# Adding transfers, one load queue and an earlier mask in the front of a fused attention and gated-convolution kernel

## The chip, the cores and the metric

The kernel runs on one core of a Trainium2 chip, in one launch. The metric is the device time of that launch in microseconds. Times before: 495.88 us median of 3 runs, 494.71 to 499.05.

## The reference

q, k and v are 4 x 8 x 576 x 64 (batch, head, position, width) in single precision. Each head adds two attentions: a pooled one, on q, k, v averaged over groups of 4 positions (144 of them), its result repeated 4 times; and a local one, where a position sees only keys less than 4 away. The 8 heads are joined to x, 4 x 576 x 512. Then two gated layers, their weights in double precision:

```
out_d = sm_attn(q_d, k_d, v_d)                       # q_d = mean of 4 rows, and so on
scores = np.where(abs(i - j) < 4, scale * q @ k.T, -1e9)
x = repeat(out_d, 4) + softmax(scores) @ v
h = relu(x @ w_in);  x = (h * sigmoid(conv3(h))) @ w_out          # 512 -> 1024 -> 512
out = (sigmoid(conv5(x)) * (x @ w_val)) @ w_out2                  # 512 -> 512 -> 512
```

## The kernel before

Attention is done in 16 steps (4 batches x 4 pairs of heads). A step loads k and q (`load`), turns them on TensorE (`transp`), copies them out of PSUM on ScalarE (`evac`), pools them on VectorE (`pooled`), and runs the pooled attention (`down_s` to `down_o`) and the local one (`loc_s` to `loc_o`). Local scores are made in blocks of 24 positions by 32 keys; the mask is a tile that TensorE adds first (`loc_s`, `identr` times `maskr`). GpSimd makes the mask (lines 832 to 848: one memset, twelve selections), and VectorE copies it to `maskr`. Local values come as windows of v in `ldw` tiles (`load_vw`, for the first batch `load_vw_first`: 24 transfers of 64 KB, 12 from SP, 12 from GpSimd). Pooled v is made by `pool_v`: one load of all four rows of a group, two additions on VectorE.

The large products take every operand as a high and a low part and sum three products (`mm3`). The high part is a ScalarE copy to the short format, the low part what is left of the value, subtracted on VectorE (`parts`; for weights `Weights.pieces`). A weight block of 512 columns by 128 rows is loaded as double precision into a stage (`Weights.load`, four stages, later three, in tiles that batches 1 to 3 use later on), and turned to single precision by one ScalarE and four VectorE instructions (`sign_off`, `to_f32`); then come the high part and the low part. There are 16 such blocks for `win` and `wout`. The first four are loaded from SP's queue, the other twelve from GpSimd's, each as soon as its stage is free.

The order of the work is written out by hand for the first four steps: `FRONT` is a list of piece names (tpk0: transpose k of step 0; pv: pool v; ab, cv, hi, lo: the four pieces of a weight block; xn, xo: the two halves of a step's output sum), and `ordered` keeps TensorE, VectorE and ScalarE in that order. GpSimd's and SP's instructions aren't held by it, they are placed by the framework's scheduler. Behind the list, steps 4 to 15 run in 8 slots each (`att_slots`), and after every slot `due_at` says how many units of the two layers' products (`ab_units`: for each batch 16 units A, x by w_in, then 16 units B, by w_out) have to have been issued. At the units in `SPLITS` the next weight block is converted and another load is issued. Behind step 15 only products of the layers are left.

Loads of the first batch go to tiles of their own; from the second batch on, `ldk`, `ldq`, `ldw` and `ldv` have one buffer each. k, q and v of step 4 are loaded ahead of `FRONT` and once more by the pieces of step 3.

Of the kernel before, what the change touches and what calls it, by code (L numbers as in the profile page):

```python
# [63 lines left out]
def kernel(  # L64
# [89 lines left out]
            return call  # L154

    vec, act = Noted(nc.vector, "vec"), Noted(nc.scalar, "act")

    def ordered(fn, engines=("pe",)):

# [31 lines left out]
    class Weights:  # L191
# [5 lines left out]
            self.staged = []  # L197
            self.n = 0

        def load(self, queue=nc.gpsimd):  # L200
            if not self.jobs:
                return
            dst, src, r0, nr, c0 = self.jobs.pop(0)
            wide = PW // nr
            rows = src[r0 * 128 : (r0 + nr) * 128]
            t, w = self.stage(self.n)
            self.n += 1
            if src.dtype == F32:
                queue.dma_start(
                    out=w.rearrange("p (r n) -> p r n", r=nr),  # L210
                    in_=rows.rearrange("(r p) n -> p r n", p=128)[:, :, c0 : c0 + wide],
                )
            else:
                queue.dma_start(
                    out=t.rearrange("p (r n) -> p r n", r=nr),
                    in_=rows.bitcast(I32).rearrange("(r p) n -> p r n", p=128)[
                        :, :, 2 * c0 : 2 * (c0 + wide)
                    ],
                )
            self.staged.append((t, w, src.dtype == F32, dst, r0, nr, c0))  # L220
# [7 lines left out]
        def pieces(self, job):  # L228
            t, w, plain, dst, r0, nr, c0 = job
            hi, lo = (d[:, r0 : r0 + nr, c0 : c0 + PW // nr] for d in dst)  # L230
            wr = w.rearrange("p (r n) -> p r n", r=nr)
            words = t.rearrange("p (n t) -> p n t", t=2)
            return (
                lambda: plain or sign_off(act, w, words),
                lambda: plain or to_f32(vec, w, words),
                lambda: act.activation(out=hi, in_=wr, func=AF.Copy),
                lambda: vec.tensor_tensor(out=lo, in0=wr, in1=hi.bitcast(F32), op=ALU.subtract),
            )


    actx = ExitStack()
    ap = actx.enter_context(tc.tile_pool(name="ap", bufs=2))
    T, Y = {}, {}

    def load_v(b, hp):
        t = ap.tile([HD, 2, 2, 4, D], F32, tag="ldv", name="ldv", bufs=1)
        nc.sync.dma_start(
            out=t.rearrange("p e s r d -> p e s (r d)"),
            in_=v[b, 2 * hp : 2 * hp + 2].rearrange("h (s p r) d -> p h s (r d)", s=2, r=4),
        )  # L250
        T["ldv", b, hp] = t

    first = {}

    def load(src, tag, b, hp):

        if b == 0:
            slot = f"hg{'hi' if tag == 'ldk' else 'lo'}{hp}"
            t = mp.tile([QT, 2, NT, D], F32, tag=slot, name=tag)
            nc.sync.dma_start(  # L260
                out=t.rearrange("p e t d -> p e (t d)"),
                in_=src[b, 2 * hp : 2 * hp + 2].rearrange("h (p t) d -> p h (t d)", p=QT),
            )
        else:
            t = ap.tile([QT, NT, 2, D], F32, tag=tag, name=tag, bufs=1)
            for e in range(2):
                nc.sync.dma_start(
                    out=t[:, :, e, :], in_=src[b, 2 * hp + e].rearrange("(t p) d -> p t d", p=QT)
                )
        T[tag, b, hp] = t  # L270

    def load_v_first(part):

        if part == 0:
            first["v"] = keep.tile([HD, H, 2, 4, D], F32, tag="wout1", name="ldv")
        n = H // 2
        t = first["v"][:, part * n : part * n + n]
        nc.sync.dma_start(
            out=t.rearrange("p h s r d -> p (h s) (r d)"),
            in_=v[0, part * n : part * n + n].rearrange("h (s p r) d -> p (h s) (r d)", s=2, r=4),  # L280
        )
        for hp in range(part * HP // 2, (part + 1) * HP // 2):
            T["ldv", 0, hp] = first["v"][:, 2 * hp : 2 * hp + 2]

    def load_vw_first(queue, blocks):

# [32 lines left out]
    ROWS = [slice(64 * e, 64 * e + 64) for e in range(2)]  # L319

    def pool_v(s):
        b, hp = where(s)
        vq = T.pop(("ldv", b, hp))
        t2 = vq[:, :, :, 0:2]
        vec.tensor_tensor(out=t2, in0=t2, in1=vq[:, :, :, 2:4], op=ALU.add)
        vd = ap.tile([HD, 2, 2, D], F32, tag="vd", name="vd")
        vec.tensor_tensor(out=vd, in0=t2[:, :, :, 0], in1=t2[:, :, :, 1], op=ALU.add)
        T["vd", s] = vd

    def transp(s, name):  # L330
        src = T.pop(("ld" + name, *where(s)))
        p = pair("tp")
        inrow = src.shape[1] == 2
        for i in range(NT):
            to = p[:, i // 3, i % 3 * QT : i % 3 * QT + QT]
            if inrow:
                for e in range(2):
                    mm(to[ROWS[e]], src[:, e, i], ident[:QT, :QT], start=True, stop=True)
            else:
                mm(to, src[:, i].rearrange("p e d -> p (e d)"), ident[:QT, :QT], is_transpose=True)  # L340
        T["tp" + name, s] = p, inrow

    def evac(s, name):
        p, inrow = T.pop(("tp" + name, s))
        t = ap.tile([128, S], F32, tag=name + "T", name=name + "T", bufs=1)
        if inrow:
            to = t.rearrange("c (p s i) -> c p s i", s=2, i=3)
            pv = p[:, :, : 3 * QT].rearrange("c s (i p) -> c p s i", i=3)
        else:
            to, pv = t.rearrange("c (s p) -> c s p", s=2), p[:, :, : 3 * QT]  # L350
        act.activation(out=to, in_=pv, func=AF.Copy, scale={"k": scale, "q": 1.0}[name])
        T[name + "T", s] = t
# [202 lines left out]
    def where(s):  # L555
        return s // HP, s % HP

    def att_slots(s):
# [22 lines left out]
            put(7, s, down_av, down_o)  # L581
        if s + 1 < NSTEP:
            put(4, s + 1, lambda s: prep(s, "k"), lambda s: load_vw(*where(s)))
            put(5, s + 1, lambda s: prep(s, "q"), pool_v, next_v)
        return P

    XO = []

    def next_load(s, name):
        if HP <= s + 1 < NSTEP:  # L590
            load({"k": k, "q": q}[name], "ld" + name, *where(s + 1))

    def next_v(s):
        if HP <= s + 1 < NSTEP:
            load_v(*where(s + 1))

    def prep(s, name):
        transp(s, name)
# [226 lines left out]
    for hp in range(2):  # L825
        load(k, "ldk", 0, hp)
        load(q, "ldq", 0, hp)
    load_v_first(0)
    load_vw_first(nc.sync, (0, 1))
    for h in HT:  # L830
        nc.gpsimd.memset(h, 0.0)
    nc.gpsimd.memset(mask, 0.0)
    m3 = mask[:, : NG * KB].rearrange("p (g k) -> p g k", k=KB)
    spans = [(c, 0, NG, 4) for c in range(4)]
    spans[0] = (0, 1, NG - 1, 4)
# [1 line left out]
    for c, g, n, off in spans + [(0, 0, 1, 0), (3, NG - 1, 1, QB * (NB - 1) - key_start(NB - 1))]:  # L837
        m = m3[32 * c : 32 * c + 32, g : g + n]
        for sgn in (1, -1):
            nc.gpsimd.affine_select(  # L840
                out=m,
                in_=m,
                compare_op=ALU.is_ge,
                fill=BIG,
                base=3 - sgn * off,
                pattern=[[0, n], [sgn, KB]],
                channel_multiplier=-sgn,
            )
    vec.tensor_copy(identr, ident)
    vec.tensor_copy(maskr, mask)  # L850
    load_vw_first(nc.gpsimd, (2, 3))

    def stage(n):
        tag = ("y1", "y2", "y3", "g")[n % 4] if n < 9 else ("y2", "y3", "g")[n % 3]
# [9 lines left out]
    for hp in range(2, HP):  # L864
        load(k, "ldk", 0, hp)
        load(q, "ldq", 0, hp)
        if hp == 2:
            load_v_first(1)
    for _ in range(4):
        W.load(nc.sync)  # L870
    nw = 3 * KF + 5 * KM
# [13 lines left out]
        T["cw"] = pair("cw")[:, 0]  # L885
        mm(T["cw"][:, :nw], cwf, ident[:nw, :nw], is_transpose=True)

    load_v(1, 0)
    load(k, "ldk", 1, 0)
    load(q, "ldq", 1, 0)  # L890
    stream = [fn for b in range(B) for fn in ab_units(b)]
# [3 lines left out]
    def due_at(n):  # L895
# [4 lines left out]
        if n > 32:  # L900
            return n
        n += 4
        return n * 16 // 14 if n < 14 else 16 + (n - 14) * 16 // 22

    def step_unit():

# [21 lines left out]
                behind(conv5_e, 1, e)  # L928

    ALL = ("pe", "vec", "act")  # L930
    SPLITS = (0, 2, 4, 6, 8, 10, 12, 14, 16, 18, 20, 22)
    FRONT = """
        tpk0 tpq0 kT0 kd0 qT0 pv0 sl0 qd0 pv1 sd0 mxl0 tpq1 mxd0 sub0 xd0 tpk1 qT1 smd0 scd0 qd1
        kT1 etd0 xl0 kd1 sl1 sml0 etc0 mul0 tr0 sd1 mxl1 sub1 avd0 mxd1 xl1 sml1 xd1 tpq2 mul1 pv2
        od0 avl0 qT2 smd1 scd1 qd2 avm0 xn0 tpk2 xo0 tr1 xhi0 xlo0 etd1 kT2 kd2 sl2 etc1 ab0 cv0
        sd2 avd1 mxd2 hi0 tpq3 ab1 mxl2 xd2 sub2 lo0 pv3 od1 tpk3 qT3 xl2 smd2 qd3 ab2 scd2 sml2
        avl1 mul2 kT3 etd2 xn1 kd3 ab3 avm1 cv1 etc2 sd3 xo1 hi1 sl3 mxd3 xhi1 tr2 xd3 xlo1 avd2
        mxl3 cwa0 smd3 tpk4 od2 sub3 scd3 cv3 avl2 xl3 kT4 avm2 xn2 hi3 etd3 sml3 xo2 tpq4 etc3
        mul3 xhi2 tr3 avd3 cv2 qT4 od3 avl3 cwv0 hi2 avm3 xn3 xlo2 cwp0 xo3 cwc0 xhi3 lo3 xlo3 lo2
        lo1 pv4 qd4 kd4  # L940
    """.split()

    def by_name():

        F = {}
        for s in range(HP + 1):
            for name, fn in dict(
                tpk=lambda s: (transp(s, "k"), next_load(s, "k"), load_vw(*where(s)) if s == HP else 0),
                tpq=lambda s: (transp(s, "q"), next_load(s, "q")),
                kT=lambda s: evac(s, "k"),  # L950
                qT=lambda s: evac(s, "q"),
                kd=lambda s: pooled(s, "k"),
                qd=lambda s: pooled(s, "q"),
                pv=lambda s: (pool_v(s), next_v(s)),
                sl=loc_s,
                mxl=loc_m,
                sub=loc_d,
# [118 lines left out]
```

## Time and profile before

| | |
|---|---|
| median of 3 runs | 495.88 us (494.71 to 499.05) |
| profiled execution | 497.79 us, its span 496.0 us, granted TensorE clock 0.921 |
| TensorE products busy | 449.8 us (91%) |
| TensorE weight loads busy | 415.2 us (84%) |
| VectorE busy | 362.0 us (73%) |
| ScalarE busy | 266.4 us (54%) |
| GpSimd busy | 22.1 us (4%) |
| DMA | 39.59 MB in 69620 packets, mean 80 GB/s |
| chain that ended last | TensorE 58%, VectorE 23%, ScalarE 9%, DMA 5%, issue 4% |

Busy times of matmuls are modelled, so a TensorE that is 91% busy is not at 91% of its peak. A share over the whole span mixes stages with different limits; the chain of waits and the busy times of single stretches tell them apart. In the rows, PE is TensorE, PEld its weight loads, DVE VectorE, ACT ScalarE, POOL GpSimd, and SPq, POOLq the queues that issue transfers. Nearly all instructions carry the line of a helper (L141, L151), so a piece is known by the tiles it writes and reads.

### The profile page before, as it was taken

The page shows a single profiled execution, that of the slowest core. Times are in us where ns is not written, and L with a number is a line of the kernel's source. Part 1 is how long each engine was busy: PE and PEld are TensorE (multiplying, and loading weights), DVE is VectorE, ACT ScalarE, POOL GpSimd, SP SyncE. Part 2 cuts the span into 40 slices and gives each one's busy share as a digit, 9 for nine tenths or more (in the row PEclk, how much of TensorE's full clock was granted, in tenths as well). Part 3 has the DMA queues.
Part 4 walks back from the last instruction along what each step waited for, and adds up shares of the span by engine and source line. Part 5 has one row for each costly group of instructions (what it writes and reads, how often), then busy time and mean ns, then how long its engine had stood idle before and what let it go on. Part 6 is the DMA issues. An engine that isn't in the chain of part 4 may idle for free.

```text
span 496.0 us, 13820 instructions
## 1 busy us (share of the span) xinstructions
PE 449.8 (91%) x5961; PEld 415.2 (84%) x5961; DVE 362.0 (73%) x655; ACT 266.4 (54%) x564; POOL 22.1 (4%) x49
## 2 busy tenths in 40 slices
PE   3669995987798999999999999999979999999997
PEld 3469885976698998987999988899979999889985
DVE  0588998999976458898857998338999775939530
ACT  2357637677554356784654976426684443635221
POOL 7200010101100000000000000000000000000000
PEclk9985558878777999999999999999999999999999
DMA  9994443424341431413314121142101000210102
GB/s 192 204 256 121 84 155 93 130 64 111 113 123 29 97 78 32 104 29 78 79 35 100 36 48 34 34 166 91 44 1 44 0 1 21 86 65 22 65 23 106
DMA packets 69620, 39.59 MB, mean 80 GB/s; under 512 B 55978, under 2 KB 64502, under 8 KB 69558
## 3 DMA queue, kind: packets, MB, share of 16 engines
q1 hardware_dynamic: 67446, 31.62, 25.3%
q0 software_dynamic: 2112, 7.08, 4.6%
q8 instruction: 47, 0.77, 0.6%
q14 instruction: 15, 0.12, 0.1%
HBM read 33.96 MB, written 4.72 MB: 78 GB/s over the span
## 4 chain that ended last, share of the span: by engine, by line
PE 58%; DVE 23%; ACT 9%; DMA 5%; issue 4%; POOL 1%; POOLq 0%; DVEq 0%; ACTq 0%
PE pb L141 20%; PE pc L141 10%; PE pd L141 10%; DVE cv L151 8%; PE pa L141 7%; PE avl L141 4%; DMA ldv<-in_v_dram 3%; DVE stage L151 3%; PE tp L141 2%; DVE hglo L151 2%; ACT ed L151 2%; ACT cv L151 2%; ACT h L151 2%; DMA ldw<-in_v_dram 2%; PE sl L141 1%
## 5 line engine op out<-in xcount | busy, mean ns | idle before, releaser
L141 PE MATMUL pb<-hghi,wout 128*128 128x288 f32 x512 | 105.6, 316 | 3.9 <-ACT hghi L151 3.9
L141 PE MATMUL pa<-xhi,win 128*128 128x288 f32 x512 | 104.4, 313 | 0.0
L141 PEld LDWEIGHTS pb<-hghi,wout 128*128 128x128 f32 x512 | 81.7, 200 | 7.1 <-ACT hghi L151 4.4
L141 PEld LDWEIGHTS pa<-xhi,win 128*128 128x128 f32 x512 | 80.2, 197 | 3.0 <-issue 2.3
L141 PE MATMUL pb<-hglo,wout 128*128 128x288 f32 x256 | 57.6, 307 | 0.5 <-DVE hglo L151 0.5
L141 PE MATMUL pa<-xlo,win 128*128 128x288 f32 x256 | 56.6, 304 | 0.0
L151 DVE SCALAR_TENSOR_TENSOR cv<-h,cwt,cv 128x576 f32<-128x576 f32 x64 | 51.3, 810 | 5.4 <-ACT cv L151 5.1
L141 PEld LDWEIGHTS pc<-ys,wval 128*128 128x128 f32 x384 | 51.6, 188 | 0.6
L141 PE MATMUL pc<-ys,wval 128*128 128x288 f32 x384 | 52.0, 294 | 0.0
L151 DVE SCALAR_TENSOR_TENSOR g<-y,cwt,g 128x576 f32<-128x576 f32 x64 | 49.8, 810 | 0.3
L141 PEld LDWEIGHTS avl<-et,ldw 32*64 32x64 f32 x1536 | 31.0, 164 | 20.1 <-issue 14.1
L141 PE MATMUL avl<-et,ldw 32*64 32x24 f32 x1536 | 34.0, 237 | 13.9 <-issue 8.4
L141 PE MATMUL pd<-wout,hghi 128*128 128x512 f32 x144 | 45.3, 395 | 0.0
L141 PEld LDWEIGHTS pb<-hglo,wout 128*128 128x128 f32 x256 | 43.7, 200 | 1.0 <-DVE hglo L151 1.0
L141 PEld LDWEIGHTS pa<-xlo,win 128*128 128x128 f32 x256 | 43.2, 198 | 0.0
L151 ACT ACTIVATE ed<-sd,mxd 72x144 f32<-72x144 f32 x64 | 23.2, 370 | 21.1 <-DVE mxd L151 21.0
L141 PEld LDWEIGHTS pd<-wout,hghi 128*128 128x128 f32 x144 | 26.8, 188 | 5.9
L151 ACT ACTIVATE cv<-cv 128x576 f32<-128x576 f32 x32 | 21.9, 683 | 15.5 <-DVE cv L151 15.2
L151 ACT ACTIVATE hghi<-gvf 128x576 fp32r<-128x576 f32 x16 | 11.0, 686 | 34.0 <-DVE gvf L151 34.0
L141 PE MATMUL pd<-wout,hglo 128*128 128x512 f32 x72 | 28.0, 395 | 0.0
L151 DVE SCALAR_TENSOR_TENSOR cv<-cv,h 128x576 f32<-128x576 f32 x32 | 23.8, 749 | 4.6 <-ACT cv L151 4.4
L151 DVE SCALAR_TENSOR_TENSOR gvf<-g,pc 128x576 f32<-128x576 f32 x16 | 11.9, 752 | 20.5 <-PE pc L141 20.5
(90 smaller groups left out, 712.9 us busy)
## 6 DMA issues: line engine op xcount, KB each, us to landing
out_dram<-o SPq DMA_DIRECT2D x18, 256.0 KB
stage<-in_moe_w_out_dram POOLq DMA_DIRECT2D x8, 512.0 KB, 3.8
ldv<-in_v_dram SPq DMA_DIRECT2D x13, 288.0 KB
ldk<-in_k_dram SPq DMA_DIRECT2D x26, 144.0 KB
ldq<-in_q_dram SPq DMA_DIRECT2D x26, 144.0 KB
ldw<-in_v_dram SPq DMA_DIRECT2D x48, 48.0 KB
stage<-in_moe_w_in_dram SPq DMA_DIRECT2D x4, 512.0 KB
stage<-in_moe_w_in_dram POOLq DMA_DIRECT2D x4, 512.0 KB, 5.9
```

Of the source, the lines that this page charges most:

```text
L141: last["pe"] = nc.tensor.matmul(*a, **kw)
L151: last[self.key] = getattr(self.engine, name)(*a, **kw)
```

## The change

The low part of a weight block is made by a ScalarE copy that writes minus the high part and by a transfer, issued by GpSimd, that adds the value onto it in place. v is pooled in the same way from step 2 on: four transfers, the first plain and the other three adding, bring the four rows of each group onto one another (`sum_v`); steps 2 and 3 share one chain, and `vd` gets three buffers. Steps 0 and 1 still use `pool_v`. All stages are loaded from SP. On GpSimd the mask comes ahead of everything but the identity; a quarter of the first windows (instead of half), the sum of v for steps 2 and 3 and the memsets of `h` come behind it; SP gets three quarters of the windows. k and q of steps 2 and 3 are loaded with both heads interleaved, in runs of 256 bytes, so that a transposition takes both heads at once, in its own mode instead of as a product with the identity. k, q and v of step 4 are loaded once. `FRONT`, `SPLITS` and `due_at` are new.

```
+    pool = Noted(nc.gpsimd, "pool")
...
-        def load(self, queue=nc.gpsimd):
+        def load(self, queue=nc.sync):
...
-                lambda: vec.tensor_tensor(out=lo, in0=wr, in1=hi.bitcast(F32), op=ALU.subtract),
+                lambda: self.low_part(wr, hi, lo),
             )
+
+        @staticmethod
+        def low_part(w, hi, lo):
+
+            act.activation(out=lo, in_=hi.bitcast(F32), func=AF.Copy, scale=-1.0)
+            nc.gpsimd.dma_start(out=lo.bitcast(F32), in_=w, accum_op=ALU.add)
...
         if b == 0:
             slot = f"hg{'hi' if tag == 'ldk' else 'lo'}{hp}"
+            if hp < 2:
...
+            else:
+                t = mp.tile([QT, NT, 2, D], F32, tag=slot, name=tag)
+                for e in range(2):
+                    nc.sync.dma_start(
+                        out=t[:, :, e, :], in_=src[b, 2 * hp + e].rearrange("(p t) d -> p t d", p=QT)
+                    )
...
+    def sum_v(b, hp, n=2):
+
+        t = ap.tile([HD, n, 2, D], F32, tag="vd" if n == 2 else "vd4", name="vd", bufs=3 if n == 2 else 1)
+        rows = v[b, 2 * hp : 2 * hp + n].rearrange("h (s p r) d -> p (h s) r d", s=2, r=4)
+        for r in range(4):
+            nc.gpsimd.dma_start(
+                out=t.rearrange("p h s d -> p (h s) d"),
+                in_=rows[:, :, r],
+                **({"accum_op": ALU.add} if r else {}),
+            )
...
-            put(5, s + 1, lambda s: prep(s, "q"), pool_v, next_v)
+            put(5, s + 1, lambda s: prep(s, "q"), next_v)
...
     def next_load(s, name):
-        if HP <= s + 1 < NSTEP:
+        if HP < s + 1 < NSTEP:
             load({"k": k, "q": q}[name], "ld" + name, *where(s + 1))
 
     def next_v(s):
-        if HP <= s + 1 < NSTEP:
-            load_v(*where(s + 1))
+        if HP < s + 1 < NSTEP:
+            sum_v(*where(s + 1))
...
-    load_v_first(0)
-    load_vw_first(nc.sync, (0, 1))
-    for h in HT:
-        nc.gpsimd.memset(h, 0.0)
-    nc.gpsimd.memset(mask, 0.0)
+    load_v_first()
+    load_vw_first(nc.sync, (0, 1, 2))
+    pool.memset(mask, 0.0)
...
-            nc.gpsimd.affine_select(
+            pool.affine_select(
...
-    load_vw_first(nc.gpsimd, (2, 3))
+
+    def behind_masks():
+        load_vw_first(nc.gpsimd, (3,))
+        sum_v(0, HP // 2, H // 2)
+        for h in HT:
+            nc.gpsimd.memset(h, 0.0)
+
+    ordered(behind_masks, ("pool",))
...
-    load_v(1, 0)
+    sum_v(1, 0)
     load(k, "ldk", 1, 0)
     load(q, "ldq", 1, 0)
...
-        return n * 16 // 14 if n < 14 else 16 + (n - 14) * 16 // 22
+        return n * 16 // 12 if n < 12 else 16 + (n - 12) * 16 // 24
...
-    SPLITS = (0, 2, 4, 6, 8, 10, 12, 14, 16, 18, 20, 22)
+    SPLITS = (0, 2, 4, 6, 11, 13, 15, 17, 19, 21, 23, 25)
     FRONT = """
...
+        tpk0 tpq0 kT0 kd0 qT0 qd0 sl0 sd0 mxl0 sub0 tpq1 mxd0 xl0 sml0 xd0 mul0 tpk1 smd0 qT1 qd1
+        scd0 pv0 kT1 etd0 kd1 sd1 tr0 etc0 pv1 sl1 mxd1 xd1 avd0 mxl1 sub1 smd1 od0 scd1 avl0 avm0
+        xl1 xn0 sml1 etd1 xo0 mul1 etc1 tpq2 tr1 xhi0 tpk2 qT2 xlo0 qd2 avd1 kT2 kd2 sl2 od1 sd2
+        mxl2 sub2 avl1 mxd2 xl2 xn1 xd2 avm1 sml2 tpq3 smd2 ab0 xo1 scd2 tpk3 mul2 tr2 cv0 qT3
+        etd2 kT3 etc2 sl3 xhi1 kd3 hi0 qd3 avd2 lo0 mxl3 ab2 sub3 sd3 od2 xlo1 xl3 ab3 mxd3 avl2
+        ab1 xd3 xn2 avm2 sml3 tpq4 cwa0 smd3 mul3 scd3 tpk4 xo2 tr3 xhi2 cv1 etd3 qT4 etc3 kT4
+        avd3 xlo2 hi1 cv2 od3 lo1 avl3 avm3 xn3 hi2 qd4 lo2 xo3 kd4 xhi3 xlo3 cv3 cwv0 hi3 lo3
+        cwp0 cwc0
...
-                tpq=lambda s: (transp(s, "q"), next_load(s, "q")),
+                tpq=lambda s: (transp(s, "q"), next_load(s, "q"), next_v(s)),
...
-                pv=lambda s: (pool_v(s), next_v(s)),
+                pv=pool_v,
```

## Rows read from the trace of the kernel before

**Rows 1.** Busy by stretch: length; PE, PEld, DVE, ACT, POOL; clock, DMA share, GB/s.

```profile
0.00:16.00 16.00, 4.11 (x48) 3.84 (x48) 0.33 (x2) 2.58 (x3) 12.64 (x33) 1.00 0.96 189
16.00:34.00 18.00, 12.76 (x380) 10.88 (x381) 14.46 (x34) 8.83 (x31) 0.00 (x0) 0.95 1.07 249
34.00:70.00 36.00, 34.48 (x774) 30.21 (x772) 32.21 (x70) 19.36 (x51) 3.02 (x4) 0.50 0.47 107
70.00:150.00 80.00, 65.59 (x862) 61.00 (x860) 73.41 (x143) 51.49 (x109) 6.10 (x9) 0.81 0.40 116
150.00:335.00 185.00, 178.73 (x2930) 165.79 (x2929) 131.12 (x249) 106.98 (x247) 0.22 (x2) 0.98 0.26 65
```

**Rows 2.** Time line, 0 to 34 us: start, length, engine, line, output from input, count, idle before.

```profile
3.16 12.75 SPq L293 DMA_DIRECT2D ldw<-in_v_dram  x12
4.15 2.19 PE L141 MATMUL tp<-ident,ldk 96*64 96x96 f32 x24 [4.15 <-DMA ldk<-in_k_dram]
6.37 0.65 ACT L151 ACTIVATE kT<-tp 128x576 f32<-128x576 f32 x1 [4.35 <-PE tp L141]
13.72 2.15 POOL L840 TENSOR_SCALAR_AFFINE_SELECT mask<-mask 32x160 f32<-32x160 f32 x6
15.90 0.29 DVE L151 CAST maskr<-mask 128x256 fp32r<-128x256 f32 x1 [13.05 <-POOL mask L840]
19.43 7.14 SPq L214 DMA_DIRECT2D stage<-in_moe_w_in_dram  x4
32.29 2.39 PE L141 MATMUL avl<-et,ldw 32*64 32x24 f32 x96 [3.93 <-issue]
33.85 0.46 DVE L151 TENSOR_TENSOR xo<-avl,od 128x288 f32<-128x288 f32 x1 [0.49 <-PE avl L141]
```

**Rows 3.** Time line of VectorE where the written-out front ends.

```profile
68.83 0.74 DVE L151 TENSOR_REDUCE kd<-kT 128x144 f32<-128x576 f32 x1
```

**Rows 4.** Groups by line and shape, whole span: count, busy us, mean ns, idle before.

```profile
L151 DVE TENSOR_TENSOR wout<-stage,wout 128x512 fp32r<-128x512 f32 x8 | 5.5, 681 | 0.7 <-ACT wout L151 0.7
L151 DVE TENSOR_TENSOR ldv<-ldv 72x512 f32<-72x512 f32 x16 | 10.9, 683 | 6.9 <-DMA ldv<-in_v_dram 6.8
L151 DVE TENSOR_TENSOR vd<-ldv 72x256 f32<-72x256 f32 x16 | 6.7, 417 | 3.3 <-PE avd L141 2.8
L151 DVE TENSOR_REDUCE qd<-qT 128x144 f32<-128x576 f32 x16 | 11.9, 742 | 1.5 <-ACT qT L151 1.5
L151 DVE TENSOR_REDUCE sml<-el 128x12 f32<-128x384 f32 x16 | 8.7, 544 | 1.2 <-ACT el L151 1.2
L151 DVE SCALAR_TENSOR_TENSOR stage<-stage 128x512 int32<-128x512 int32 x32 | 21.8, 684 | 0.5
L151 ACT ACTIVATE wout<-stage 128x512 fp32r<-128x512 f32 x8 | 5.0, 630 | 8.6 <-DVE stage L151 8.6
```

**Rows 5.** A piece of the chain of waits that ended last: start, us, what.

```profile
185.17 3.74 DMA ldv<-in_v_dram
```

**Rows 6.** Who waited for whom, whole span: us in total, times, longest.

```profile
POOL stage L214 <- DVE win L151: 59.5, 6, 28.5
DVE ldv L151 <- DMA ldv<-in_v_dram: 6.8, 7, 1.9
```

**Rows 7.** Time line of SP's queue: the first loads in runs of 256 bytes.

```profile
29.68 2.72 SPq L267 DMA_DIRECT2D ldk<-in_k_dram  x2
```

**Rows 8.** Line 214, stage loads from GpSimd: issue, min/median/max ns; landing.

```profile
L214 POOL DMA_DIRECT2D stage<-in_moe_w_out_dram x8: 748/748/751, 76.1 to 134.6; - x8
...
DMA to landing us min/median/max: 3.6/4.0/7.2
```

**Rows 9.** Tile ldw: landing of GpSimd's window loads in the first 16 us.

```profile
DMA to landing us min/median/max: 5.0/8.1/9.3
```

**Rows 10.** Time line of TensorE: local scores of two steps, one behind the other.

```profile
148.13 0.39 PE L141 MATMUL sl<-maskr,identr 128*128 128x256 f32 x2
168.73 0.40 PE L141 MATMUL sl<-maskr,identr 128*128 128x256 f32 x2
```

More of the change, by code (lines that the diff above doesn't have):

```diff
@@ L243 @@
     T, Y = {}, {}
[L245 to L251, printed above, removed]
     first = {}
@@ L258, in load @@
             slot = f"hg{'hi' if tag == 'ldk' else 'lo'}{hp}"
[L259 to L263, printed above, removed]
+            if hp < 2:
+                t = mp.tile([QT, 2, NT, D], F32, tag=slot, name=tag)
+                nc.sync.dma_start(
+                    out=t.rearrange("p e t d -> p e (t d)"),
+                    in_=src[b, 2 * hp : 2 * hp + 2].rearrange("h (p t) d -> p h (t d)", p=QT),
+                )
+            else:
+                t = mp.tile([QT, NT, 2, D], F32, tag=slot, name=tag)
+                for e in range(2):
+                    nc.sync.dma_start(
+                        out=t[:, :, e, :], in_=src[b, 2 * hp + e].rearrange("(p t) d -> p t d", p=QT)
+                    )
         else:
@@ L270, in load, with load_v_first @@
         T[tag, b, hp] = t
-    def load_v_first(part):
-        if part == 0:
-            first["v"] = keep.tile([HD, H, 2, 4, D], F32, tag="wout1", name="ldv")
+    def load_v_first():
         n = H // 2
-        t = first["v"][:, part * n : part * n + n]
+        t = keep.tile([HD, n, 2, 4, D], F32, tag="wout1", name="ldv")
         nc.sync.dma_start(
             out=t.rearrange("p h s r d -> p (h s) (r d)"),
-            in_=v[0, part * n : part * n + n].rearrange("h (s p r) d -> p (h s) (r d)", s=2, r=4),
+            in_=v[0, :n].rearrange("h (s p r) d -> p (h s) (r d)", s=2, r=4),
         )
-        for hp in range(part * HP // 2, (part + 1) * HP // 2):
-            T["ldv", 0, hp] = first["v"][:, 2 * hp : 2 * hp + 2]
+        for hp in range(HP // 2):
+            T["ldv", 0, hp] = t[:, 2 * hp : 2 * hp + 2]
+    def sum_v(b, hp, n=2):
[6 more added lines that the diff above has]
+                **({"accum_op": ALU.add} if r else {}),
+            )
+        for i in range(n // 2):
+            T["vd", b * HP + hp + i] = t[:, 2 * i : 2 * i + 2]
     def load_vw_first(queue, blocks):
@@ L321, in pool_v @@
     def pool_v(s):
-        b, hp = where(s)
-        vq = T.pop(("ldv", b, hp))
+        vq = T.pop(("ldv", *where(s)))
         t2 = vq[:, :, :, 0:2]
         vec.tensor_tensor(out=t2, in0=t2, in1=vq[:, :, :, 2:4], op=ALU.add)
-        vd = ap.tile([HD, 2, 2, D], F32, tag="vd", name="vd")
+        vd = ap.tile([HD, 2, 2, D], F32, tag="vd", name="vd", bufs=3)
         vec.tensor_tensor(out=vd, in0=t2[:, :, :, 0], in1=t2[:, :, :, 1], op=ALU.add)
@@ L332, in transp @@
         p = pair("tp")
-        inrow = src.shape[1] == 2
         for i in range(NT):
             to = p[:, i // 3, i % 3 * QT : i % 3 * QT + QT]
-            if inrow:
+            if src.shape[1] == 2:
                 for e in range(2):
@@ L340, in transp @@
                 mm(to, src[:, i].rearrange("p e d -> p (e d)"), ident[:QT, :QT], is_transpose=True)
-        T["tp" + name, s] = p, inrow
+        T["tp" + name, s] = p
     def evac(s, name):
-        p, inrow = T.pop(("tp" + name, s))
+        p = T.pop(("tp" + name, s))
         t = ap.tile([128, S], F32, tag=name + "T", name=name + "T", bufs=1)
-        if inrow:
+        if s < HP:
             to = t.rearrange("c (p s i) -> c p s i", s=2, i=3)
@@ L866 @@
         load(q, "ldq", 0, hp)
-        if hp == 2:
-            load_v_first(1)
     for _ in range(4):
@@ L930 @@
     ALL = ("pe", "vec", "act")
-    SPLITS = (0, 2, 4, 6, 8, 10, 12, 14, 16, 18, 20, 22)
+    SPLITS = (0, 2, 4, 6, 11, 13, 15, 17, 19, 21, 23, 25)
     FRONT = """
[L933 to L940, printed above, removed]
+        tpk0 tpq0 kT0 kd0 qT0 qd0 sl0 sd0 mxl0 sub0 tpq1 mxd0 xl0 sml0 xd0 mul0 tpk1 smd0 qT1 qd1
[6 more added lines that the diff above has]
+        cwp0 cwc0
     """.split()
```

## The prediction

> **What bounds the kernel now.** I read the span by stages first [rows 1]: busy time of each engine and TensorE's granted clock in five stretches. The reader is to see three regimes. From 0 to 16 us nothing but loads and GpSimd runs (VectorE 0.33 us busy). From 16 to 150 us VectorE is nearly full: 14.46 of 18, 32.21 of 36 and 73.41 of 80 us, while TensorE stands idle 14.4 us in the last of these and has a mean clock of 0.50 (its lower level, 1.2 GHz) and then 0.81 of full speed. From 150 us on TensorE is the bound, 178.73 of 185 us at clock 0.98 up to 335 us, and VectorE has room. So VectorE's work is worth its full length only before 150 us; behind that it is worth only what it makes TensorE wait.
>
> The second view is the time line of the first 34 us [rows 2]. The first k^T is out of PSUM at 6.37 + 0.65 = 7.0 us, but VectorE and the local scores wait until 15.90 for the mask, whose last six selections GpSimd runs from 13.72, behind twelve transfers that it issues. The first output half of attention comes at 33.85. The third is where the written-out front ends: kd of step 4, VectorE's last piece of it, ends at 68.83 + 0.74 = 69.6 us [rows 3].
>
> **The change, part by part.**
>
> *Front up to the first output half.* Twelve selections take 2 x 2.15 = 4.3 us [rows 2]; put first, behind the identity, they are done near 6 us, so k^T at 7.0 releases VectorE. The 16 to 34 us stretch did 14.46 us of VectorE work; the new list puts step 1's sums and product and step 2's v and q pooling behind that point (0.9 + 0.6 + 1.1 + 0.75 = 3.4 us [rows 4]), so 11 us remain and VectorE alone would get there at 18. The loads end later: SP issued 12 window loads in 12.75 us, 1.06 each; 18 of them from 3.2 us end at 22.3, GpSimd's six go beside. With some 2 us for the last to land and its product I take 24 for the first half's sum, 9.9 us earlier than 33.85. Bounds: 18 if loads don't bind, and 30.5 if TensorE's idle 3.93 us ahead of that product, put down to issue [rows 2], comes back and the loads are slow as well.
>
> *The rest of the front.* VectorE's whole front is 14.46 + 32.21 = 46.7 us, less 0.4 behind its end = 46.3. Removed: four low parts at 0.68 = 2.7, and v of steps 2, 3 and 4 at 0.684 + 0.418 = 1.10 each, 3.3 [rows 4]. 40.3 remain, 11.4 of them before the first half, so 28.9, plus the 3.8 us that VectorE idled from 34 to 70: 24 + 28.9 + 3.8 = 56.7 in place of 69.6. Front: **-13 us**, from -15 (all of the idle time of before, 7.4 us, kept: 7.0 + 40.3 + 7.4 = 54.7) to -6.5 (first half at 30.5). TensorE was 34.48 of 36 us busy at half clock in that stretch and could have set the end instead; its k and q transposes of steps 2 and 3 fall from four groups of 24 (2.19 us for the first such group [rows 2]) to four groups of 6 wider ones, some 4 us less by my estimate, so it would end by about the same time.
>
> *The stretch from 70 to 150 us.* Twelve low parts (8.2 us) and v of about four steps (4.4) leave VectorE: 73.4 - 12.6 = 60.8. ScalarE gains twelve negated copies at 0.63 [rows 4]: 51.5 + 7.6 = 59.1. TensorE has 65.6 busy. All three would then be close to one another, so I take half of VectorE's saving, **-6 us**; bounds 0 and -12 (TensorE's 14.4 us idle cap it). The steeper release of units (16 in 12 slots instead of 14) is costed at nothing: the same units lie ahead of slot 36 either way. A higher clock there would cut TensorE's 65.6 us; I take nothing for it.
>
> *From 150 us.* VectorE waits 6.8 us in seven places for a v transfer that starts late, since its buffer is single [rows 6]; one such transfer, 3.74 us, is a piece of the chain of waits [rows 5]. They go, and 1.10 us a step. TensorE idles only 6.3 us there, mostly for other reasons: **-1 us**, 0 to -3. Behind the last attention step nothing changes.
>
> *Loads dropped.* k, q and v of step 4 came twice; the second set lay beside other work: 0. Loads of steps 2 and 3 in 256-byte runs cost SP 1.36 us each where they contended [rows 7]; eight end near 33 with the window loads ahead of them, and the four weight loads (7.14 us [rows 2]) are moved some 10 us back. The first conversion stands behind about 20 us of VectorE work, so near 33: little is late. Moved memsets: hidden, h is first written after the front.
>
> *What is added on GpSimd.* Each low part: a negated copy, an issue, a landing. Eight issues of whole blocks, the most of them beside a full VectorE, took 0.748 to 0.751 us, and such a block of 512 KB 4.0 to land (3.6 to 7.2) [rows 8]; a low part moves half. Each v: four transfers, each of which must wait for the one before to land, with GpSimd's queue standing behind the wait. The price of one adding landing stands in no row. Bounds: nothing under 0 is excluded by its replacing a load; 3.6 and, in the loaded start, 5.0 to 9.3 us (median 8.1 [rows 9]). Away from the start I take 3.74, the plain v load in the same stage [rows 5]: 4 x (0.75 + 3.74) = 18 us a step, under the 20.6 us between two steps' local scores [rows 10]. In the start the first chain takes 4 x (0.75 + 8.1) = 35 us from about 8 us on, to 43: up to 5 us late for step 2's product. I charge **+3 us** for that and for low parts held behind chains; bounds 0 and, by the rival below, over 30.
>
> The Trainium skill, DMA: Bandwidth & Descriptors, section on the anatomy of a GpSimd DMA, gives some 2.0 us plus bytes at 436 GB/s, so an estimate of 2.2 us for such a landing and 12 us a chain, under which the 3 us above would fall away and the sum be 3 us less; no row here shows one.
>
> **Sum.** -13 - 6 - 1 + 3 = -17 on the profiled execution's 497.8 us: 480.8. That execution lies 1.9 us above the median of the runs, 495.9, so I predict **479**.
>
> **Rivals.**
>
> *A, low parts hold TensorE.* Output weights are now converted 5 units ahead of use, where it was about 8; at 1.5 slots a unit and 20.6/8 = 2.6 us a slot that is 19.5 us. Sign, conversion (two steps of 0.68 and two cheaper ones, some 2.2 [rows 4]), two copies, issue and landing are 0.63 + 2.2 + 0.63 + 0.63 + 0.75 + 4.0 = 8.8; a v chain of 18 ahead makes 27, 7 us too many. Two such misses cost 14: 493, no change. For: one queue. Against: a low part need not meet a chain's start, and one wait gives the next more room. 0.11.
>
> *B, slower: GpSimd's queue becomes the bound.* If a landing takes over 5 us, a chain exceeds the step: four links of 0.75 + L against 20.6 plus about 2.5 us a step, which v loaded two steps ahead can absorb over 11 steps: L = 5.0. At L = 6 a step loses 27 - 23.1 = 3.9 us, 43 in 11 steps: 479 + 43 = 522. For: the loaded window transfers took 8.1. Against: those shared full DMA engines (0.96 in the first 16 us, 0.26 from 150 on [rows 1]). 0.13.
>
> The eight issues of [rows 8] spread by 3 ns from the least to the most at a full VectorE. The Trainium skill, SBUF — State Buffer, section on the two separate sides, says that VectorE in a two-port mode locks GpSimd out of writing descriptors (620 ns alone, 3100 beside it). By that rule a link would be near 7 us and B would hold; the trace does not agree so far.
>
> *C, loads set the start.* The first half at 30.5: -6.5 for the front, 485.5. For: DMA engines are 0.96 and 1.07 busy to 34 us [rows 1], and v by 256-byte runs adds to it. 0.13.
>
> *D, SP stands.* GpSimd waited 59.5 us in six places for the low parts to free a stage [rows 6]; SP now waits for this, with k, q and window loads behind. They have some 20 us ahead of use, 4 of it landing. Four waits of 3 us past it: 491, no change. 0.07.
>
> **How the numbers follow.** Forecast 0.56 (466 to 488 by its bounds: -30 to -8), A 0.11, B 0.13, C 0.13, D 0.07. Faster by over 1% (under 490.9; about what a measurement here can tell): forecast, C and a little of A and D, 0.72; within 1%: 0.15; slower: B and a tail of A, 0.13. The range of 465 to 494 holds all but B and the tails.
>
> **What would show it.** The mask's conversion near 6 to 7 us; the first output half near 24, kd of step 4 near 57; 96-by-64 transposes of steps 2 and 3 gone, for k and for q; VectorE busy 362 less 16 x 0.68 and 14 x 1.10, about 336; no wait for ldv after step 1. Wrong if GpSimd's adding transfers are over 5 us apart in steps 5 and on, if TensorE waits on a low part or on vd, or if SP's stage waits come ahead of late k or q.

## The result, and the profile after

The changed kernel takes 487.56 us (median of 15 runs, 483.46 to 490.72), the kernel before beside it 496.76 (15 runs): a ratio of 0.9833, 95% interval 0.9806 to 0.986. Faster, by half of what was forecast. The profiled execution took 488.81 us, its span 487.0, against 497.79 and 496.0: -9 us.

Busy time by stretch of the changed kernel, columns as in [rows 1]:

```profile
0.00:16.00 16.00, 11.11 (x210) 9.60 (x210) 7.38 (x17) 6.72 (x18) 12.00 (x30) 1.00 1.00 175
16.00:34.00 18.00, 13.40 (x304) 10.81 (x305) 9.67 (x21) 7.29 (x21) 8.07 (x8) 0.51 1.20 173
34.00:70.00 36.00, 26.83 (x644) 23.47 (x630) 27.91 (x61) 20.84 (x52) 12.23 (x11) 0.53 0.97 181
70.00:150.00 80.00, 69.40 (x986) 63.67 (x985) 63.71 (x128) 58.15 (x127) 25.37 (x22) 0.87 0.73 133
150.00:335.00 185.00, 179.73 (x2862) 167.89 (x2863) 129.12 (x237) 111.85 (x249) 29.62 (x29) 0.98 0.39 75
```

VectorE has lost work in every stretch behind the first, but from 16 to 70 us it has also lost its fullness (37.6 of 54 us busy, before 46.7), and from 34 to 70 us TensorE with it (26.83 us busy, before 34.48). From 34 to 70 and from 70 to 150 us DMA is 0.97 and 0.73 busy where it was 0.47 and 0.40.

The time line of the front and of two later steps (start, length, engine, line, output from input, count, idle before), to be laid beside [rows 2, 3, 10]:

```profile
3.17 18.71 SPq L310 DMA_DIRECT2D ldw<-in_v_dram  x18
6.67 0.29 DVE L151 CAST maskr<-mask 128x256 fp32r<-128x256 f32 x1 [4.73 <-POOL mask L151]
25.02 1.60 PE L141 MATMUL avl<-et,ldw 32*64 32x24 f32 x52 [1.84 <-DMA ldw<-in_v_dram]
25.56 0.46 DVE L151 TENSOR_TENSOR xo<-avl,od 128x288 f32<-128x288 f32 x1 [3.87 <-PE avl L141]
29.45 1.20 PE L141 MATMUL tp<-ident,ldq 96*128 96x96 f32 x6 [1.71 <-DMA ldq<-in_q_dram]
59.09 0.74 DVE L151 TENSOR_REDUCE kd<-kT 128x144 f32<-128x576 f32 x1
64.08 0.30 PE L141 MATMUL cw<-ident,cw 44*128 44x44 f32 x1 [6.50 <-DVE cw L151]
66.15 0.85 PE L141 MATMUL pa<-xhi,win 128*128 128x288 f32 x2
138.62 0.40 PE L141 MATMUL sl<-maskr,identr 128*128 128x256 f32 x2
162.12 0.40 PE L141 MATMUL sl<-maskr,identr 128*128 128x256 f32 x2
```

The mask is converted 9.2 us earlier, the first output half comes 8.3 us earlier, VectorE's last k sum 9.7 us earlier. Then TensorE stands 6.5 us for the convolution weights (`cw`), and its first layer product `pa` starts at 66.15. Before it started at 65.39:

```profile
65.39 0.85 PE L141 MATMUL pa<-xhi,win 128*128 128x288 f32 x2
```

The front has not let the layers begin earlier. The gain shows behind it: step 7's local scores start 9.5 us earlier than in [rows 10], step 8's only 6.6, the last step's (295.16 against 304.46) 9.3.

The transfers of v, 13 plain ones and 39 that add, by tile: issue in ns (min/median/max), first and last start, then landing in us:

```profile
L294 POOL DMA_DIRECT2D vd<-in_v_dram x52: 742/1178/1729, 4.4 to 267.5; - x52
DMA to landing us min/median/max: 2.3/3.6/9.9
```

and the adding transfers of the low parts, as readers of the tile `stage`:

```profile
L245 POOL DMA_DIRECT2D win<-stage x8: 1270/1275/1798, 51.9 to 100.1; - x8
L245 POOL DMA_DIRECT2D wout<-stage x8: 1277/1534/1874, 104.0 to 156.9; - x8
DMA to landing us min/median/max: 4.2/5.6/9.3
```

Who waits, over the whole span (total us, times, longest):

```profile
POOL vd L294 <- DMA vd<-in_v_dram: 86.4, 30, 7.4
SPq L215 <- DMA win<-stage: 40.7, 8, 11.7
SPq L215 <- DMA wout<-stage: 18.0, 3, 9.2
```

GpSimd stands between the links of v's chains, and SP stands until a low part has landed, because that frees the stage. Before, GpSimd stood for the stages alone [rows 6], with nothing else to do.

### The profile page after: what moved, and what is told of

The parts are those of the page before. It is cut to its first block, busy times and chain, and to the rows that moved or that the text cites. A ratio compares the mean times of both kernels' runs of the same rounds, so it can differ in the third digit from the quotient of the medians.

```text
span 487.0 us, 13782 instructions
## 1 busy us (share of the span) xinstructions
PE 445.3 (91%) x5889; PEld 409.7 (84%) x5889; DVE 341.3 (70%) x611; ACT 276.1 (57%) x580; POOL 87.4 (18%) x99
## 4 chain that ended last, share of the span: by engine, by line
PE 61%; DVE 18%; ACT 9%; DMA 7%; issue 3%; SPq 1%; ACTq 0%; DVEq 0%
PE pb L141 17%; PE pa L141 11%; PE pc L141 10%; PE pd L141 10%; DVE cv L151 7%; DVE stage L151 4%; DMA ldw<-in_v_dram 3%; PE avl L141 3%; PE tp L141 3%; PE sl L141 3%; ACT ed L151 2%; DVE hglo L151 2%; ACT cv L151 2%; DMA ldk<-in_k_dram 2%; PE avd L141 2%
## 5 line engine op out<-in xcount | busy, mean ns | idle before, releaser
L141 PE MATMUL pb<-hghi,wout 128*128 128x288 f32 x512 | 104.3, 313 | 4.3 <-ACT hghi L151 3.8
L141 PE MATMUL pa<-xhi,win 128*128 128x288 f32 x512 | 102.8, 310 | 0.0
L141 PEld LDWEIGHTS pb<-hghi,wout 128*128 128x128 f32 x512 | 80.3, 197 | 7.6 <-ACT hghi L151 4.3
L294 POOL DMA_DIRECT2D vd<-in_v_dram x52 | 58.0, 1150 | 138.6 <-DMA vd<-in_v_dram 86.4
L151 ACT ACTIVATE cv<-cv 128x576 f32<-128x576 f32 x32 | 21.8, 683 | 12.6 <-DVE cv L151 12.3
```

Of the source, the lines that this page charges most:

```text
L141: last["pe"] = nc.tensor.matmul(*a, **kw)
L151: last[self.key] = getattr(self.engine, name)(*a, **kw)
L294: nc.gpsimd.dma_start(out=t.rearrange("p h s d -> p (h s) d"), in_=rows[:, :, r], **({"accum_op": ALU.add} if r else {}),)
```

## Experiments

Each ratio is to the kernel before on the same chip.

**e1_cw_first.** The convolution weights loaded ahead of the windows and converted at step 2's transposes:

```
- load conv3, conv5 behind all loads of FRONT
+ load conv3, conv5 ahead of the windows
- FRONT: ... tpq4 cwa0 smd3 ...   cwv0 hi3 lo3 cwp0 cwc0
+ FRONT: etc1 cwa0 tpq2 tr1 xhi0 tpk2 qT2 xlo0 cwv0 qd2 avd1 cwp0 kT2 kd2 cwc0 ...
```

> The changed kernel with the 44 KB of convolution weights loaded ahead of the value windows and their conversion and transposition placed at step 2's transposes instead of last in the list. Theory 1 (the front's gain was lost at its tail: TensorE ends its list near 57.6 us and then waits 6.5 us for this conversion, behind the weight blocks): TensorE's wait before cw goes, the first product pa begins near 61 us instead of 66.2, and the whole is 3 to 5 us faster than the changed kernel, 482 to 485 against 487.6. Rival (the front's end is set by VectorE's conversions, and the transposition only shows it): pa begins no earlier than 65, 487 to 488. Second rival (the stretch behind is bound by VectorE or ScalarE and absorbs an earlier start): pa near 61, but the end moves by less than 1 us.

0.9819 (0.9769 to 0.9868), 488.79 us: as the changed kernel. `pa` starts at 62.88, 3.3 us earlier, and then this. The time line of that run, GpSimd and TensorE:

```profile
97.02 1.76 POOL L245 DMA_DIRECT2D win<-stage  x1
100.14 1.21 POOL L294 DMA_DIRECT2D vd<-in_v_dram  x1 [1.36 <-DVE cv L151]
100.88 1.79 POOL L245 DMA_DIRECT2D win<-stage  x1
108.85 1.33 PE L141 MATMUL pa<-xhi,win 128*128 128x288 f32 x4 [10.96 <-DMA win<-stage]
```

and a piece of its chain of waits (start, us, what):

```profile
100.88 7.92 DMA win<-stage
```

ScalarE's negated copy for the second low part was done at 95.6; its transfer was issued 5.3 us later, behind a link of a v chain, and took 7.92 us. That is rival A's mechanism: what the front gained, one late low part took back.

**e2_low_part_vector.** Low parts back on VectorE, all else changed:

```
- lambda: self.low_part(wr, hi, lo),
+ lambda: vec.tensor_tensor(out=lo, in0=wr, in1=hi.bitcast(F32), op=ALU.subtract),
```

> The changed kernel with the low part of the 16 weight blocks subtracted on VectorE again; all else as changed. Theory 1 (VectorE's relief counts in the stretch from 66 to 140 us, where it is full): 16 x 0.68 = 10.9 us come back on VectorE and 10 leave ScalarE; the gain of 9.5 us by step 7 falls to some 3 to 5 us and the whole is 3 to 6 us slower than changed, 491 to 494. Rival (the adding transfers cost what they save, since the stages come free later and SP stands for them, 40.7 + 18.0 us of waits): as fast as changed or up to 4 us faster, 484 to 488.

0.977 (0.9735 to 0.9804), 486.09 us: no slower, by the ratios some 0.6% faster (the intervals lie just apart), although VectorE is 72.00 us busy from 70 to 150 us instead of 63.71. Beside v's chains, the low parts' transfers gain nothing.

**e3_stage_from_gpsimd** and **e8_old_units.** `queue=nc.gpsimd` for the stages; and `due_at` and `SPLITS` of the kernel before.

> The changed kernel with the twelve waiting weight loads issued from GpSimd as before. Theory 1 with SP's standing as the loss at 135 to 152 us (TensorE waits 3.2 us for k there, and VectorE 9.5 us for stages): k comes in time, but the stage loads and the v chains now hold each other on GpSimd; within 2 us of changed, 486 to 490. Rival (SP's queue is what took back the middle's gain): 3 us faster, 484 to 485. Third (GpSimd's queue becomes the bound): slower by over 5 us, 493 or more.

> The changed kernel with the units released and the weight blocks converted as before (16 units in 14 slots, output weights 8 units ahead of use instead of 5). Theory 2 (low parts late behind v chains and late stages cost a few us at 135 to 152): the longer lead takes the waits for stages away, but VectorE gets more work early; within 2 us of changed, 486 to 490. Rival (the release of units is a large part of the gain): 4 us slower or more, 492 and up.

0.98 (0.9765 to 0.9835) and 0.9811 (0.9776 to 0.9846): both as the changed kernel. The queue of the stages and the units' release carry nothing of the result that these intervals can tell. `pa` starts at 67.72 and 67.33 here and at 68.00 in e2, all with the changed kernel's list, whose `pa` was at 66.15: these are single profiled executions, so up to 2 us of `pa` say little.

**e4_old_mask_first.** The kernel before with GpSimd's mask alone moved ahead of its transfers.

```
+ pool = Noted(nc.gpsimd, "pool")     # memset and selections through it
- load_vw_first(nc.gpsimd, (2, 3)) ahead of them
+ ordered(behind_masks, ("pool",))    # windows and memsets of h behind them
```

> The kernel before with only the mask put first on GpSimd (all window transfers and memsets behind it). Theory 1 (an early start alone is taken back within the front, where loads and TensorE at its lower clock set the pace): VectorE starts 8 to 9 us earlier, the first product pa begins 0 to 4 us earlier than 65.4, the whole 0 to 4 us faster than before, 493 to 497. Rival (the start passes through, as predicted): 8 to 9 us faster, 487 to 489.

0.994 (0.9906 to 0.9974), 495.1 us: -3 us, `pa` at 64.10. VectorE's first k sum starts 9.0 us earlier (7.09 against 16.11), but the old list has step 0's v next, and VectorE stands 5.91 us for its load. The first output half comes only 0.9 us earlier (32.95 against 33.85): most of the early start is given back at once.

**e5_cw_early_low_vector.** Edits of e2 and, with the loads behind the first windows, of e1.

> The changed kernel with the low parts on VectorE and the convolution weights loaded behind the first windows and converted at step 2's transposes. Theory 2 (an earlier end of the front does pass to the end as long as no low part waits in GpSimd's queue; the 10.96 us for a low part took it back in the run with the conversion alone): the first product pa begins 3 to 6 us earlier than the 68.0 of the run with low parts on VectorE, no wait for a low part follows, 481 to 484. Rival (VectorE, full behind the front, absorbs an earlier start): pa earlier, the end as in that run, 485 to 487.

0.9662 (0.9631 to 0.9693), 481.31 us: faster than both kernels, and than e2 by 1.1%. With no low part in GpSimd's queue the 5.4 us that `pa` gains on e2 are kept:

```profile
62.04 0.30 PE L141 MATMUL cw<-ident,cw 44*128 44x44 f32 x1 [0.71 <-DVE cw L151]
...
62.58 0.85 PE L141 MATMUL pa<-xhi,win 128*128 128x288 f32 x2
```

and in e2:

```profile
68.00 0.85 PE L141 MATMUL pa<-xhi,win 128*128 128x288 f32 x2
```

**e6_v_and_low_vector** and **e7_v_vector.** v of steps 2 and on by one load and two additions again, with the low parts on VectorE (e6) or by transfers, now alone in GpSimd's queue (e7):

```
- sum_v(...)   # four transfers, three adding
+ load_v(...)  # one buffer; pool_v in slot 5, pieces pv2, pv3, pv4 in FRONT
```

> The changed kernel without any adding transfer: low parts and v of all steps on VectorE, v loaded by SP into its single buffer; mask, list (with the pooling of v put in at steps 2, 3 and 4), units and loads as changed. Theory 2 with v's adding transfers as the part that gains (14 x 1.10 us off VectorE, four to five of them where it is full, and no wait for a v load): 4 to 7 us slower than the run with low parts alone on VectorE (486), 490 to 493. Rival (mask, list and dropped loads hold the whole gain): 485 to 488.

> The changed kernel with v of all steps on VectorE as in the run before, low parts by adding transfers, which now have GpSimd's queue to themselves. If the low part's harm is the queue behind the v chains: landings 4 to 5 us, no wait of TensorE or of a stage for them, and 2 to 5 us faster than the run without any adding transfer. Rival (the way by copy, issue and landing costs by itself, and ScalarE's copy too): as that run or slower.

e6: 1.0095 (1.0064 to 1.0126), 502.92 us, where 4 to 7 us more than e2 were expected and 16.8 were measured. e7: 1.014 (1.0085 to 1.0195), its six times from 501.52 to 511.41 us; against e6 that is no difference clear of the intervals. v's transfers are worth far more than the working gave them. Busy time by stretch of e6, two stretches of the steps 5 to 8:

```profile
94.00:124.00 30.00, 19.99 (x300) 17.88 (x298) 28.23 (x56) 18.12 (x38) 0.11 (x1) 0.78 0.35 96
...
148.00:169.00 21.00, 17.53 (x279) 16.21 (x278) 14.26 (x30) 8.53 (x23) 0.00 (x0) 0.76 0.30 75
```

and the same of e2:

```profile
94.00:124.00 30.00, 26.42 (x448) 23.69 (x447) 29.70 (x57) 21.06 (x45) 6.03 (x6) 0.91 0.45 102
...
148.00:169.00 21.00, 20.14 (x375) 18.55 (x376) 12.84 (x29) 12.29 (x36) 6.13 (x6) 1.00 0.43 71
```

With v on VectorE, TensorE is busy 6.4 and 2.6 us less in these stretches, and its granted clock is lower as well (0.78 against 0.91, 0.76 against 1.00 of the upper level).

**e10_old_v_transfers** and **e11_old_low_transfers.** One part alone on the kernel before: v's transfers (`sum_v` behind GpSimd's windows, three `vd` buffers, pv2 to pv4 out of the list, v of step 4 loaded once), or the low parts' (`low_part`).

> The kernel before with v of steps 2 to 15 pooled by adding transfers, and nothing else: mask, windows, list, units, low parts, stages as before, the pieces pv2, pv3, pv4 taken out of the list. Theory 3 (v's transfers are the part that gains: 14 steps at 1.10 us of VectorE, seven waits of 6.8 us in all for v): 484 to 490. Rival (they gain only with the new list and the early mask, since GpSimd's twelve windows and the mask now stand ahead of the first chain): 494 to 499.

> The kernel before with the 16 low parts made by a negated copy and an adding transfer, and nothing else; the stage loads stay on GpSimd's queue beside them. Theory 3 (the low part's transfer costs more than the 0.68 us of VectorE that it takes away): 497 to 504. Rival, the price of the prediction (16 x 0.68 us off a full VectorE): 488 to 493.

e10: 0.9743 (0.9714 to 0.9773), 487.35 us: v's transfers alone give more than the whole change, with the old list and the late mask. Step by step the gain comes late: `pa` starts at 67.27, 1.9 us later than before, step 8's local scores 8.4 us earlier (160.33), the last step's 10.0 us earlier (294.46 against 304.46). Two stretches of e10:

```profile
94.00:124.00 30.00, 25.32 (x464) 23.09 (x460) 29.97 (x58) 22.55 (x47) 9.88 (x11) 1.00 0.50 118
...
148.00:169.00 21.00, 21.00 (x424) 19.57 (x422) 11.41 (x29) 11.29 (x35) 5.46 (x5) 1.00 0.41 67
```

and of the kernel before:

```profile
94.00:124.00 30.00, 24.12 (x331) 22.35 (x330) 29.47 (x58) 20.72 (x44) 3.11 (x5) 0.84 0.41 117
...
148.00:169.00 21.00, 19.49 (x307) 18.06 (x305) 10.28 (x22) 7.93 (x21) 0.00 (x0) 0.84 0.28 67
```

TensorE's busy time hardly differs (+1.2, +1.5 us), its clock does (0.84 to 1.00 in both). Busy time by mean clock, a rough measure of work done, is 20.3 + 16.4 = 36.6 before and 25.3 + 21.0 = 46.3 in e10: 9.7 us more in these 51. That this is near the 10.0 us of the last step proves nothing, as the stretches are two of several and of one execution each. Against the clock as the cause: e4, only 0.6% faster, also has 1.00 from 148 to 169 us (TensorE busy 19.63), and e10's two executions of 487.32 and 487.38 us had mean clocks of 0.974 and 0.926 over the whole span.

Besides VectorE's time, v's transfers do away with the loads into the single buffer `ldv`, which start when it comes free. The chain of waits of the kernel before goes over four of them, these three and the one in [rows 5], 14.8 us in all:

```profile
95.04 4.62 DMA ldv<-in_v_dram
...
206.25 3.21 DMA ldv<-in_v_dram
...
266.42 3.23 DMA ldv<-in_v_dram
```

In e10's chain there is none of them. VectorE itself stood 6.8 us for such loads [rows 6], so the chain overstates what they cost. How much of e10's gain is VectorE's time, how much these waits and how much the clock stays open; a second `ldv` buffer in the kernel before was not run.

e11: 1.0116 (1.0077 to 1.0155), 505.57 us: 1.2% slower. Its chain of waits shows the price; pieces of it (start, us, what):

```profile
126.48 4.19 DMA wout<-stage
...
131.25 0.49 POOL stage L214
132.01 6.00 DMA wout<-stage
...
138.59 5.09 DMA stage<-in_moe_w_out_dram
143.71 0.66 ACT stage L151
```

A low part lands, its stage is free, the stage's load lands, and only then can the conversion begin: the landing stands in series with the load, where VectorE's 0.68 us stood before. Both issues are in GpSimd's queue here, so the queue has a share in this too.

**e9_v_one_transfer** and **e12_v_one_low_vector.** Of each v chain the plain transfer alone, so that v isn't averaged, the rest as changed (e9) or as in e2 (e12):

```
- for r in range(4):
+ for r in range(1):
```

> The changed kernel with the first, plain transfer of each v chain alone; the three adding ones are left out, so v isn't averaged and 'vd' holds every fourth row. Prices what the chains (four waits in GpSimd's queue) still cost. Theory 3 (v's chains are off the path, and the low parts by transfers are dear by themselves: a copy, an issue of 1.27 us, a landing of 5.6 us and a stage held longer): 486 to 489, as the changed kernel. Rival (low parts stand behind v's chains, and that is what eats the gain): 480 to 484, and from step 7 on no ScalarE wait for a stage over 3 us.

> The changed kernel with both edits: v by its first, plain transfer alone (the three adding ones left out, so v isn't averaged), and the low parts subtracted on VectorE. With the changed kernel, the second and the ninth run it makes a square. Theory 4 (the chains, standing in GpSimd's queue and on the DMA engines, take back what the low parts' transfers gain; without the chains these transfers do free VectorE): slower than the ninth run, a ratio of 0.970 to 0.977, 482 to 486 by a before of 497.5. Rival (low parts by transfers gain nothing even beside single v transfers, and the chains are dear wherever the low parts are made): a ratio of 0.957 to 0.964, 476 to 480.

e9: 0.9619 (0.9586 to 0.9653), 481.04 us, as its rival had it, though one ScalarE wait for a stage was over the 3 us named (3.58, in the changed kernel 4.75). e12: 0.9662 (0.9608 to 0.9715), 482.4 us: below theory 4's range and above its rival's, so neither size held. As a square: the chains cost 2.1% beside low parts by transfers (0.9833 to 0.9619) and 1.1% beside low parts on VectorE (0.977 to 0.9662). The first number's excess, 1.1 points and uncertain by some 0.8, would be the meeting of the two in one queue. Whether the low parts' transfers gain anything when no chain is there is not settled: 0.9619 and 0.9662 have overlapping intervals, and e7 and e11, also without chains but with v on VectorE, were slow. The time line of e9, GpSimd:

```profile
95.77 1.27 POOL L245 DMA_DIRECT2D win<-stage  x1 [4.10 <-ACT win L151]
...
149.26 1.27 POOL L245 DMA_DIRECT2D wout<-stage  x1 [8.92 <-ACT wout L151]
```

Here GpSimd waits for ScalarE's copy. In the changed kernel these two were issued at 100.06 and 156.92, the first 4 us after its copy was done.

## Why the prediction was wrong in its largest term

**Start up to the first half: right.** The mask at 6.67 (near 6 to 7), SP's windows ending at 21.9 (22.3), the half's sum at 25.56 (24); -8.3 us of -9.9. The loads end the wait for it, as in the working. The mask alone doesn't do it (e4: -0.9 us). The new list puts v behind step 0's sums; which of the other edits brought the rest was not run apart.

**"Front: -13 us": the step that failed.** The number was taken at VectorE's last k sum, 69.6 before; that came at 59.8, near the 56.7 forecast. But before, TensorE began the layers at 65.39, 4 us ahead of VectorE's end, so VectorE's end wasn't what the front delivers. And the new list has two pieces behind that sum that stood ahead of it before, the conversion of a weight block (`cv3`) and that of the convolution weights: VectorE reached the second at 62.84, TensorE had ended its own list at 57.6 and waited. VectorE left the front 5 us earlier (64.6 against 69.6), TensorE 0.8 us later. The idle time was underrated too: from the first half's sum to the last k sum the working had 28.9 us of work and 3.8 idle, VectorE was busy 26.3 and idle 8.0, with a q load that the chain holds for 5.21 us from 24.10 and a TensorE at 0.50 of its clock. e5 shows the order at fault: the conversion earlier gives 5.4 us at `pa` and 1.1% of the time against e2, once the low parts don't take it back. The prediction had named TensorE as a possible end of the front and set it aside on an estimate of its transposes, without asking what in the list its first layer product waits for.

**The low parts: wrong in sign.** 16 x 0.68 us were to leave a full VectorE. VectorE did lose 9.7 us from 70 to 150 (forecast 12.6, with v), yet e2 is no slower with them back, and e11, the low parts' transfers alone, is 5.8 us slower by its ratio. The sum priced the issue at 0.75 and the landing at 4.0 us [rows 8] and had nothing for the stage that waits for them, which only rival D named; they are 1.27 to 1.53 and 5.6, and they stand ahead of the stage's next load.

**v: right in kind, far under in size.** The working counted 1.10 us a step and 6.8 us of waits [rows 6], 22 us in 14 steps, and kept some 6.5: 3.3 in the front, half of 4.4 from 70 to 150, 1 behind. e10 gives -2.6%, about 13 us, e6 16.8 against e2. In e10 10.3 us of it come between `pa` and step 8, where the working kept the half of 4.4, and 1.6 behind step 8, where it had 1. The landing held (3.6 us in the median, 3.74 taken), and no `ldv` wait is left behind step 1. Of TensorE's clock, for which the working took "nothing", two stretches of e10 show the upper level (1.00) where it was 0.84; that the gain comes from it isn't shown.

**From 70 us on** the sum was -6 - 1 + 3 = -4; measured is -9.8 (+0.8 at `pa`, -9.0 at the end), of which VectorE's 5 us out of the front are a part. That the time, 487.56 us, still lies inside the forecast's 466 to 488 is luck: the front's missing gain was made up in part by v's. The bound of -8 there does not follow from the working either: its weak ends, -6.5, 0, 0 and +3, add up to -3.5.

By single parts on the kernel before: v -2.6%, low parts +1.2%, mask -0.6%; their sum, -2.0%, is near the -1.7% of the whole, but the parts don't simply add. e2, all of the change but the low parts (0.977), is no faster than e10, v's transfers alone (0.9743): beside v's transfers, mask, list, loads and units together gave nothing that the intervals can tell. e6, which has them without v's transfers, is 1% slower than the kernel before; its places for v's pieces in the new list are one choice of many.

**The rivals.** B didn't come: a median landing of 3.6 us, 3.3 from 150 to 335 us, lies under the 5.0 from which it decides, though single links of steps 7 and 8 were 5.8 and 8.0 us apart, over the 5 us named as a sign of being wrong. The estimate by the Trainium skill, DMA: Bandwidth & Descriptors, section on the anatomy of a GpSimd DMA, was 2.2 us a landing; the median here is 3.6, and 2.2 is near the least, 2.3. By the rule of the Trainium skill, SBUF — State Buffer, section on the two separate sides, a GpSimd transfer beside a VectorE copy in a two-port mode takes some 3.1 us instead of 0.62. No issue of v's 52 took that long (1.18 in the median, 1.73 at most); whether VectorE was in such a mode beside one, no run here shows. A is real (e1); in the changed kernel TensorE's longest wait for a low part is 0.6 us, and the list that began the layers earlier brought the 10.96. C missed: the loads bind, but not at 30.5. D came in small. A piece of the chain of waits of the changed kernel:

```profile
144.53 7.61 DMA ldk<-in_k_dram
```

and, on TensorE's time line, the wait that it ends in:

```profile
152.27 1.19 PE L141 MATMUL tp<-ident,ldk 96*128 96x96 f32 x6 [3.21 <-DMA ldk<-in_k_dram]
```

SP had stood for a stage until 135.04 and issued twelve window transfers, half of this k and one more stage load before it came to the rest of k. These are the 3 us lost between steps 7 and 8. D's place was right. In e3, whose SP loads only the first four stages, the same transposition starts without a wait:

```profile
152.20 0.71 PE L141 MATMUL tp<-ident,ldk 96*128 96x96 f32 x6
```

and step 8 1.9 us earlier than in the changed kernel, but the whole, 0.98 against 0.9833, is not clear of it.

## What to carry to other kernels

A front's worth is read where the next stage's first instruction starts, so list what that instruction waits for and put it early; the end of the busiest engine is another mark. Work moved off a full engine onto a transfer must be priced to its landing and to what the landing frees, and a chain of dependent transfers shares its queue badly with transfers that others wait for. Try the parts alone: here one part gave more than the whole.

## What was not expected of the hardware

A v transfer takes GpSimd 1.18 us to issue in the median, with 39 of 52 adding; the 13 plain ones alone took 0.75 in e9. The low parts' adding transfers take 1.27 to 1.53 us, plain stage loads 0.75. TensorE, busy 11.11 of the first 16 us instead of 4.11, ran at 0.51 of its full clock from 16 to 34 us, busy 13.40 of 18 us, where it had 0.95 before, busy 12.76. That the early work lowered it isn't shown: e11, busy 4.05 of the first 16 us, had 0.50 from 16 to 34 us too. Nor does the busy time of a stretch settle the clock: from 148 to 169 us TensorE was busy 19.49 of 21 us with 0.84 in the kernel before, and 19.63 with 1.00 in e4.
